# A fused attention and MoE kernel: a third quarter of one block in seven products, w_out loaded four neighbouring rows to a partition, and w_in's columns taken four apart

## The chip, the core and the metric

The kernel runs on one core of a Trainium2 chip. The metric is the device time of one execution in microseconds. The kernel before took 202.1 us, the median of three runs (201.06 to 202.36). TensorE (PE) multiplies, PEld is its loading of weights, VectorE (DVE), ScalarE (ACT) and GpSimd (POOL) work element by element, and SyncE (SP) issues DMAs; ScalarE and GpSimd issue DMAs as well.

## The reference

Linear attention with a decay per head over q, k, v of (4 batches, 8 heads, 768 positions, 64), in blocks of 64 positions, then a two-layer network over the 3072 tokens of 512 features.

```python
for b in range(nb):                              # blocks of 64 positions
    qb, kb, vb = (q[:, :, sl], k[:, :, sl], v[:, :, sl])
    intra = np.einsum('bhic,bhjc->bhij', qb, kb) * Dmask[None]
    intra = np.einsum('bhij,bhjd->bhid', intra, vb)
    inter = np.einsum('bhid,bhde->bhie', qb * lam_pow[None], kv_state)
    out[:, :, sl] = intra + inter
    kv_state = lam_block * kv_state + np.einsum('bhsd,bhse->bhde', kb * rev_pow[None], vb)
x = out.transpose(0, 2, 1, 3).reshape(B * S, H * D)      # 3072 x 512
h = x @ w_in                                             # 512 x 2048
return (h / (1 + np.exp(-h))) @ w_out                    # 2048 x 512
```

The hidden features (the 2048 columns of w_in and rows of w_out) may be taken in any order, as long as both matrices take the same.

## The kernel before

**Staging.** The 768 positions of a batch are six units of 128; with four batches there are 24 units of 128 tokens. They are worked in twelve sets of two units. For each set SyncE loads q, k and v (L411 for the first four sets, whose transfers carry runs of 512 bytes; L416 for the others), VectorE and ScalarE cast and scale them to bf16 (`kq`, `vd`), TensorE transposes (`tr`, L559 and L746; later sets by a DMA, L755), computes states `d_ps` (L581, L780) and scores `st_ps` (L634, L790), VectorE masks the scores (`st`), and TensorE makes the attention output `x_ps` (L660, L665, L812, L820). It is copied to `xt`, the transposed input of the first product. Between units the state is carried in `xf` and, as a block matrix, in `xe`.

**First product.** The tokens are in eight groups: four of 256 tokens (the first four sets) and four of 512 tokens. `product1` (L941 on) computes, for a group, the 16 tiles of 128 hidden features with four matmuls each, over the 512 input features (L958); ScalarE applies silu from PSUM into `g` (L973). For the last group, and for the half of the group before it named by `MIXED`, `product1_spared` (L1040 on) does a block product of 2 x 2 blocks with seven products in place of eight (`A11` to `A22` are quarters of w_in, `S1` to `S4` sums of them made by VectorE in `sums_of_w_in`, `B11` to `T4` quarters and sums of `xt`). One call of its loop, a quarter of a group, has seven products of four matmuls of 256 columns (L1079), the copies and additions between them (`m`, `h`) and four silus (L1103).

**Second product.** The first four units are done plainly (`product2_plain`, L996), the other 20 in five groups of four with seven products each (`products_of`, L1209), with sums of w_out's quarters made by VectorE and results stored from `osb` by ScalarE and SyncE.

**Weights.** `w_in_bf` holds w_in as 128 partitions x 4 x 2048 in bf16, `w_out_bf` holds w_out as 128 partitions x 16 x 512. GpSimd issues their DMAs, which cast from f32, in `load_w` (L437, L440): w_in in four chunks of 512 columns, w_out in four transfers of 512 rows. Before, tile number m of the hidden features is the 128 neighbouring columns 128 m to 128 m + 127 of w_in and the same rows of w_out, so that in each w_out transfer a partition takes four rows that lie 128 rows apart. `SEQUENCE` gives the order of all loads (`s` a set, `i` a chunk of w_in, with `a` and `b` for its halves, `o` a transfer of w_out, `@` a wait for an earlier load). On GpSimd the waits are small copies into `gate` (L391): the w_in loads wait for a load of the second set, the last two w_out transfers for k of the third set. Each set is loaded q first, then k, then v, for the first four sets.

**Order.** Nothing is issued in the order in which it is written. Every step is a task with a key, the engines that may do it, assumed costs, and the buffers it takes. `Planner.order` (L65) plays the tasks through once when the kernel is built, with assumed costs for engines and DMA transfers, gives each to an engine, and emits them in the order that results. On the chip each engine then runs its instructions in exactly that order; semaphores hold an instruction until its inputs are there. While TensorE has no task early on, the planner inserts fillers: four multiplications of the identity (L1295). The constants `LEAD`, `LAZY`, `HOLD`, `ON`, `POOLS` and others set keys, buffers and the planner's choices.

```python
w_in_r = moe_w_in.rearrange("(ko p) f -> p ko f", p=128)
w_out_r = moe_w_out.rearrange("(ko p) f -> p ko f", p=128)
...
nc.gpsimd.dma_start(out=w_in_bf[:, ks, cs], in_=w_in_r[:, ks, cs])
...
nc.gpsimd.dma_start(out=w_out_bf[:, ks, :], in_=w_out_r[:, ks, :])
...
nc.tensor.matmul(t[:, j, :], lhsT=w_in_bf[:, ko, 128 * (m1 + j):128 * (m1 + j) + 128],
                 rhs=xt[gi].tile[:, ko, :], start=ko == 0 and (j == 0 or len(kos) == KI),
                 stop=True, skip_group_check=True)
```

Of the kernel before, what the change touches and what calls it, by code (L numbers as in the profile page):

```python
# [11 lines left out]
AL = mybir.AluOpType  # L12
# [206 lines left out]
def kernel(  # L219
# [24 lines left out]
    PAIRED = 2  # L244
    SETS = [[(0, b), (1, b)] for b in range(B)] + [[(n, b), (n, b + 1)] for n in range(PAIRED, NB) for b in (0, 2)]
    GROUPS = SETS[:4] + [[(n, b) for b in range(B)] for n in range(PAIRED, NB)]
    FRESH, TURNED, ALONE, LEAD = 4, 6, 6, 4.25
    SEQUENCE = "s0 s1 i0a@1.1 i0b i1a i1b i2a i2b i3a i3b o0 o1 s2@1.0 o2 o3 s3 s4"
    POOLS = dict(bank=8, ra=3, rb=6, kq=3, kqT=3, vd=3, st=3, xe=6, xf=3, y=2, yf=2,
                 xt2=2, xt4=2, g=18, s=12, m=3, osb=3, one=3, two=8, att=6, sp=2)  # L250
    BY_POOL, PLAIN = (), 4
    CASTING, SUMS_AFTER, HURRY, SUMS_ON, HOLD, ONTO = 12, 16, 0.0, 9.0, 1, 24
    EARLY, PACE = 1.0, 1.0
    OPEN, FILLED, SCALED = 4, True, (1,)
    QUERIES = (0, 1, 2, 3)
# [177 lines left out]
    def load_w(key, what, j, part):  # L433
        def go(e):
            if what == "i":
                cs, ks = slice(512 * j, 512 * j + 512), {"": slice(0, 4), "a": slice(0, 2), "b": slice(2, 4)}[part]
                nc.gpsimd.dma_start(out=w_in_bf[:, ks, cs], in_=w_in_r[:, ks, cs])  # L437
            else:
                ks = slice(4 * j, 4 * j + 4)
                nc.gpsimd.dma_start(out=w_out_bf[:, ks, :], in_=w_out_r[:, ks, :])  # L440

        t = pool_task(add((key, 0), {"POOL": 0.8}, go, [], [], 0.5243 if part else 1.0486,
                          PIECE if part else LARGE, prior=pool_last[-1:], late=TAIL))
        wload.setdefault((what, j), []).append(t)
        for h in ("a", "b") if not part else part:
            wload[what, j, h] = t
# [233 lines left out]
    def prepare(si):  # L680
# [44 lines left out]
        def scale_v(e, j):  # L725
            if e != "DVE":
                for h in range(H):
# [4 lines left out]
        cv = [add((s - 0.8, 0), by_act("v", si, j), lambda e, j=j: scale_v(e, j),  # L732
                  deps=lv, bufs=[rs[2], o.vd]) for j in range(nb)]
        after("v", cv)
        o.cv, o.ck = cv, ck

# [110 lines left out]
    def after_first(o, t):  # L847

        n, bs, nb, s = o.n, o.bs, o.nb, o.s
        w = 512 * nb // 2  # L850

        def mask(e, p):
            tt(e, o.st_of()[:, p].rearrange("p b m i -> p (b m) i"), o.st_ps[p].tile.rearrange("p b m i -> p (b m) i"),
               tri[:, None, :].to_broadcast([128, nb * NP, 64]), AL.mult)

        o.masked = [add((s - 0.9, 0), {"DVE": 0.15 + w / 950}, lambda e, p=p: mask(e, p), deps=[t], bufs=[o.st_ps[p], o.st])
                    for p in range(2)]
        after("m", o.masked)
# [82 lines left out]
    def product1(gi, tiles=None):  # L941
# [5 lines left out]
        for m0 in tiles or range(0, KO, 2 * per):  # L947
            g = Buf("g")
            for half in range(2):
# [4 lines left out]
                def mm(e, kos, bank=bank, m1=m1):  # L954
                    t = tile_of(bank, [128, per, n], F32, "h_ps")
                    for j in range(per):
                        for ko in kos:
                            nc.tensor.matmul(t[:, j, :], lhsT=w_in_bf[:, ko, 128 * (m1 + j):128 * (m1 + j) + 128],  # L958
                                             rhs=xt[gi].tile[:, ko, :], start=ko == 0 and (j == 0 or len(kos) == KI),
                                             stop=True, skip_group_check=True)  # L960

# [78 lines left out]
    def product1_spared(gi, wbufs, wdone, parts):  # L1040
# [23 lines left out]
        for jp in parts:  # L1064
# [20 lines left out]
            def keep(pool, deps, P=P, bank_of=bank_of):  # L1085
                b = Buf(pool)
                t = add((u0 - eager, 5), {"ACT": 0.6, "DVE": 0.69}, lambda e: copy(e, tile_of(b, [128, 2, 256], F32, "m"), bank_of(P)),
                        deps=deps, bufs=[b, P])
                return b, t

            narrow = {"22": Buf("vd" if closing else "y"), "12": Buf("st" if closing else "y")}

            def h_of(x, narrow=narrow):
                return tile_of(narrow[x], [128, 2, 256], F32, "h")

            def total_of(x, kept, deps, R=R, bank_of=bank_of, h_of=h_of, narrow=narrow):
                return add((u0 - eager, 5), {"DVE": 0.7}, lambda e: tt(e, h_of(x), bank_of(R), kept.tile, AL.add), deps=deps,
                           bufs=[R, kept, narrow[x]])

            def silu(dst, src, deps, bufs):  # L1100
                def go(e):
# [10 lines left out]
            m6 = product(2, P, "S2", "T2", False, [c1])  # L1112
            b2, c2 = keep("kqT" if closing else "kq", [m6])
            m5 = product(3, R, "S1", "T1", True, [s11])
            m7 = product(4, P, "S3", "T3", False, [c2])
            b3, c3 = keep("xf" if closing else KEPT, [m7])
            e22 = total_of("22", b3, [m5, c3])
            m4 = product(5, P, "A22", "T4", False, [c3])
            m3 = product(6, R, "S4", "B22", False, [e22])
            e12 = total_of("12", b2, [m3, c2])  # L1120
            s22 = silu((high, hi), lambda h_of=h_of: h_of("22"), [e22], [narrow["22"]])
            s21 = silu((high, lo), lambda P=P, f=bank_of: f(P), [m4], [P])
            s12 = silu((low, hi), lambda h_of=h_of: h_of("12"), [e12], [narrow["12"]])
# [208 lines left out]
```

## Time and profile before

| | |
|---|---|
| median of three runs | 202.1 us (201.06 to 202.36) |
| profiled execution, its own time | 201.3 us |
| span of its instructions | 199.6 us |
| TensorE matmuls | 187.6 us busy, 2607 |
| weight loads | 143.7 us busy, 2623 |
| VectorE / ScalarE / GpSimd | 145.6 / 122.3 / 13.2 us busy |
| DMA | 32.89 MB in 84894 packets |
| queue 1 (SyncE), queue 0 (GpSimd), queue 10 (ScalarE) | 75074, 4288, 5506 packets |

Busy times are shares of one execution's span. Matmuls are pipelined, and their ends are modelled: the pace of TensorE is read from how many matmuls stand in a piece of the chain and how long the piece is, and not from the duration of one. In the chain of waits each piece is given by its start, its length and what ran in it. In a timeline a piece has its start, its length, the engine, the line, the operation and what it writes and reads; what stands in brackets is how long the engine was idle before it, and what ended that. The stretches give, for each, its length and the busy time of each engine in it with the number of instructions, the granted TensorE clock as a share of full speed, the share of the DMA engines and GB/s.

### The profile page before, as it was taken

Reading aid. Unit: us, or ns where it says so; the run is one execution under the profiler, and the core shown is the slowest. Engines: PE = TensorE matmul, PEld = TensorE weight load, DVE = VectorE, ACT = ScalarE, POOL = GpSimd, SP = SyncE. Lnnn points to the kernel's source line nnn. Section 1 sums busy time; section 2 is a strip of 40 time slices with the busy share of each in tenths; the row PEclk is TensorE's granted clock in tenths of the full one; section 3 lists DMA queues with packets and bytes.
Section 4 is the critical chain, followed back from the end, with each engine's and each line's share of the span. In section 5 each row is a group of like instructions: output and inputs, shape, how many; then the busy total and the mean of one; then the engine's idle time right before and its main releaser. Section 6 shows DMA issues by size and latency. Waiting matters only on the chain.

```text
span 199.6 us, 6042 instructions
## 1 busy us (share of the span) xinstructions
PE 187.6 (94%) x2607; PEld 143.7 (72%) x2623; DVE 145.6 (73%) x302; ACT 122.3 (61%) x230; POOL 13.2 (7%) x35
## 2 busy tenths in 40 slices
PE   0699999999999998999999999999999999999993
PEld 0588687547777884667778747488887588888882
DVE  7899220279997999949999774999979763837611
ACT  2867767319896846647291574834795849765320
POOL 6086003000000000000000000000000000000000
PEclk9999999999999999999999999999999999999999
DMA  5999999999999999999989999802911001003213
GB/s 154 290 241 194 213 216 217 275 216 246 248 276 211 220 251 166 266 193 219 275 183 218 219 251 184 186 7 72 143 53 56 3 0 53 3 6 104 95 38 131
DMA packets 84894, 32.89 MB, mean 165 GB/s; under 512 B 62852, under 2 KB 84356, under 8 KB 84868
## 3 DMA queue, kind: packets, MB, share of 16 engines
q1 hardware_dynamic: 75074, 22.55, 56.0%
q0 software_dynamic: 4288, 4.20, 12.8%
q10 hardware_dynamic: 5506, 5.77, 8.9%
q8 instruction: 20, 0.33, 0.7%
q14 instruction: 6, 0.05, 0.1%
HBM read 27.26 MB, written 6.29 MB: 168 GB/s over the span
## 4 chain that ended last, share of the span: by engine, by line
PE 79%; DMA 8%; DVE 8%; POOL 1%; SPq 1%; issue 1%; ACT 0%; POOLq 0%
PE o_ps L1209 29%; PE h_ps L958 27%; PE h_ps L1079 9%; PE o_ps L996 6%; DMA w_in_bf<-in_moe_w_in_dram 4%; DMA raw<-in_q_dram 4%; PE x_ps L820 2%; PE d_ps L780 1%; DVE st L369 1%; DVE kq L369 1%; SPq L411 1%; POOL w_in_bf L437 1%; DVE xe L364 1%; PE st_ps L790 1%; PE x_ps L812 1%; PE tr L559 1%
## 5 line engine op out<-in xcount | busy, mean ns | idle before, releaser
L958 PE MATMUL h_ps<-xt,w_in_bf 128*128 128x256 bf16 (+1 forms) x407 | 66.2, 313 | 1.6 <-ACT xe L362 0.6
L958 PEld LDWEIGHTS <-w_in_bf 128*128 128x128 bf16 x416 | 39.3, 98 | 21.8 <-DVE xt L364 1.2
L973 ACT ACTIVATE g<-h_ps 128x512 bf16<-128x512 f32 x72 | 41.6, 596 | 16.8 <-PE h_ps L958 13.4
L1209 PEld LDWEIGHTS <-g 128*128 128x128 bf16 x320 | 31.2, 98 | 4.7
L1209 PEld LDWEIGHTS <-s 128*128 128x128 bf16 x240 | 23.4, 98 | 3.2
L369 DVE TENSOR_TENSOR st<-st_ps,tri 128x512 bf16<-128x512 f32 x32 | 20.3, 682 | 3.9 <-PE st_ps L790 3.9
L369 DVE TENSOR_TENSOR osb<-o_ps,m 128x512 f32<-128x512 f32 (+1 forms) x18 | 10.7, 599 | 15.8 <-ACT m L362 8.0
L362 ACT ACTIVATE m<-o_ps 128x512 f32<-128x512 f32 (+1 forms) x18 | 9.4, 522 | 18.8 <-PE o_ps L1209 18.7
L369 DVE TENSOR_TENSOR kq<-raw,lam_q 128x512 bf16<-128x512 f32 x24 | 15.9, 685 | 5.1 <-DMA raw<-in_q_dram 4.8
L369 DVE TENSOR_TENSOR vd<-raw,lam_v 128x512 bf16<-128x512 f32 x24 | 15.8, 686 | 4.7 <-DMA raw<-in_v_dram 4.6
L1209 PE MATMUL o_ps<-w_out_bf,s 128*128 128x256 bf16 x160 | 19.1, 273 | 0.0
L1209 PE MATMUL o_ps<-wsum,g 128*128 128x256 bf16 x160 | 18.9, 273 | 0.0
L1209 PE MATMUL o_ps<-w_out_bf,g 128*128 128x256 bf16 x160 | 18.6, 273 | 0.0
L362 ACT ACTIVATE xt<-x_ps 128x512 bf16<-128x512 f32 x16 | 9.8, 642 | 9.0 <-PE x_ps L820 6.1
L996 PE MATMUL o_ps<-w_out_bf,g 128*128 128x512 bf16 x57 | 14.1, 380 | 0.6 <-issue 0.3
L369 DVE TENSOR_TENSOR h<-h_ps,m 128x512 f32<-128x512 f32 x12 | 8.3, 690 | 8.0 <-PE h_ps L1079 3.7
L362 ACT ACTIVATE kqT<-tr 128x512 bf16<-128x512 bf16 x20 | 10.8, 595 | 2.3 <-PE tr L559 2.2
L362 ACT ACTIVATE kq<-raw 128x512 bf16<-128x512 f32 x16 | 9.9, 625 | 1.9 <-DMA raw<-in_k_dram 1.9
L1079 PEld LDWEIGHTS <-wsum 128*128 128x128 bf16 x96 | 9.4, 98 | 1.1
L996 PEld LDWEIGHTS <-g 128*128 128x128 bf16 x64 | 5.9, 98 | 5.5
L369 DVE TENSOR_TENSOR s<-g 128x512 bf16<-128x512 bf16 x20 | 8.3, 420 | 2.1 <-ACT g L973 1.4
L1209 PE MATMUL o_ps<-wsum,s 128*128 128x256 bf16 x80 | 9.6, 273 | 0.0
(93 smaller groups left out, 241.4 us busy)
## 6 DMA issues: line engine op xcount, KB each, us to landing
raw<-in_q_dram SPq DMA_DIRECT2D x12, 512.0 KB, 7.2
raw<-in_k_dram SPq DMA_DIRECT2D x12, 512.0 KB, 7.7
raw<-in_v_dram SPq DMA_DIRECT2D x12, 512.0 KB, 8.1
out_dram<-osb ACTq DMA_DIRECT2D x20, 256.0 KB, 3.9
w_in_bf<-in_moe_w_in_dram POOLq DMA_DIRECT2D x8, 256.0 KB, 9.4
w_out_bf<-in_moe_w_out_dram POOLq DMA_DIRECT2D x4, 512.0 KB, 14.5
out_dram<-osb ACTq DMA_DIRECT2D x4, 128.0 KB, 1.7
out_dram<-osb SPq DMA_DIRECT2D x4, 128.0 KB, 1.7
```

What stands on the lines that cost most here:

```text
L362: nc.scalar.activation(o, i, AF.Copy)
L364: nc.vector.tensor_copy(o, i)
L369: (nc.vector if e == "DVE" else nc.gpsimd).tensor_tensor(o, a, b, op=op)
L411: nc.sync.dma_start(out=rs[i].tile.rearrange("p h e d -> p h (e d)"), in_=x[i])
L437: nc.gpsimd.dma_start(out=w_in_bf[:, ks, cs], in_=w_in_r[:, ks, cs])
L559: nc.tensor.transpose(t[:, m, a], o.kq_of()[:, i, m, a], ident)
L820: nc.tensor.matmul(x_of(c)[:, j, m, :], lhsT=o.xe[c].tile[:, (bs[0] + j) % 2, m, :], rhs=o.kqT_of()[:, 1, j, m, halves[c]], start=False, s ...
L958: nc.tensor.matmul(t[:, j, :], lhsT=w_in_bf[:, ko, 128 * (m1 + j):128 * (m1 + j) + 128], rhs=xt[gi].tile[:, ko, :], start=ko == 0 and (j = ...
L973: nc.scalar.activation(t[:, half * per:half * per + per], bank.tile, AF.Silu)
L996: nc.tensor.matmul(t, lhsT=g.tile[:, j, 128 * gp:128 * gp + 128], rhs=w_out_bf[:, ko, :], start=(ko == 0), stop=(ko == KO - 1))
L1079: nc.tensor.matmul(t[:, j, :], lhsT=W[w]()[:, k2, f:f + 128], rhs=X(r)[:, k2, :], start=first and j == 0 and k2 == 0, stop=True, skip_grou ...
L1209: nc.tensor.matmul(t[:, i_, :], lhsT=src(j)[:, k2, 128 * r:128 * r + 128], rhs=W[w]()[:, 2 * j + k2, :], start=first and i_ == 0 and j == ...
```

## The change

Hidden features change places. In a chunk of 512, tile m now holds the columns m % 4, m % 4 + 4, m % 4 + 8 and so on of w_in, and the four rows of w_out that a partition takes in one transfer are neighbours in memory. Both products use the same order, so the result is that of the reference. The sums of w_in's quarters keep their layout and are read with the same step of four.

The third quarter of the group before the last (`MIXED`) is done in seven products. The order of w_in's chunks is 0, 3, 1, 2, the last two in one transfer each. Some constants of the planner change. The scaling of the carried state (`next_states`) may go to ScalarE for units 3 and 4 of a batch. `scale_pair` and the branch for `SHARED` are added but not used, as `WHOLE` and `SHARED` are empty.

```diff
-    FRESH, TURNED, ALONE, LEAD = 4, 6, 6, 4.25
-    SEQUENCE = "s0 s1 i0a@1.1 i0b i1a i1b i2a i2b i3a i3b o0 o1 s2@1.0 o2 o3 s3 s4"
+    FRESH, TURNED, ALONE, LEAD = 4, 6, 6, 4.5
+    SEQUENCE = "s0 s1 i0a@1.1 i0b i3a i3b i1 i2 o0 o1 s2@1.0 o2 o3 s3 s4"
     POOLS = dict(bank=8, ra=3, rb=6, kq=3, kqT=3, vd=3, st=3, xe=6, xf=3, y=2, yf=2,
-                 xt2=2, xt4=2, g=18, s=12, m=3, osb=3, one=3, two=8, att=6, sp=2)
+                 xt2=2, xt4=2, g=18, s=12, m=3, osb=3, one=4, two=8, att=6, sp=2)
-    CASTING, SUMS_AFTER, HURRY, SUMS_ON, HOLD, ONTO = 12, 16, 0.0, 9.0, 1, 24
+    CASTING, SUMS_AFTER, HURRY, SUMS_ON, HOLD, ONTO = 12, 16, 0.0, 9.0, 0, 24
-    LAZY, FINE, SAFE, EASY, TAIL, SURE = 2.0, True, 1.3, -0.22, 0.9, 1.5
+    LAZY, FINE, SAFE, EASY, TAIL, SURE = 0.5, True, 1.3, -0.22, 0.9, 1.5
-    MIXED, APART, KEPT = (0, 1), 1, "yf"
-    EAGER, CALM, ON = 10.0, 1.0, 0.0
+    MIXED, APART, KEPT = (0, 1, 2), 1, 'yf'
+    EAGER, CALM, ON = 10.0, 1.0, 2.0
+    SHARED = ()
+    WHOLE = ()
+    RATED = (3, 4)
...
-    w_out_r = moe_w_out.rearrange("(ko p) f -> p ko f", p=128)
+    w_out_r = moe_w_out.rearrange("(j p k) f -> p j k f", p=128, k=4)
+
+    def columns(m):
+        return slice(512 * (m // 4) + m % 4, 512 * (m // 4) + 512, 4)
...
-                nc.gpsimd.dma_start(out=w_out_bf[:, ks, :], in_=w_out_r[:, ks, :])
+                nc.gpsimd.dma_start(out=w_out_bf[:, ks, :], in_=w_out_r[:, j])
...
-        tf = add((s - 0.9, 4), {"DVE": dcost}, lambda e: tt(e, xf_of(), y.tile, rate, AL.mult),
-                 deps=[ty], bufs=[y, xf_n])
+        def next_states(e):
+            if e == "DVE":
+                tt(e, xf_of(), y.tile, rate, AL.mult)
+                return
+            for m in range(NP):
+                by_rate(e, xf_of()[:, :, m], y.tile[:, :, m], lam_be[:, m:m + 1])
+
+        tf = add((s - 0.9, 4), {"DVE": dcost, **({"ACT": 1.1} if n in RATED else {})}, next_states, deps=[ty], bufs=[y, xf_n])
...
-                            nc.tensor.matmul(t[:, j, :], lhsT=w_in_bf[:, ko, 128 * (m1 + j):128 * (m1 + j) + 128],
+                            nc.tensor.matmul(t[:, j, :], lhsT=w_in_bf[:, ko, columns(m1 + j)],
...
-                        f = 128 * (2 * jp + j)
+                        f = columns(2 * jp + j)
...
-                            nc.tensor.matmul(t[:, j, :], lhsT=W[w]()[:, k2, f:f + 128], rhs=X(r)[:, k2, :],
+                            nc.tensor.matmul(t[:, j, :], lhsT=W[w]()[:, k2, f], rhs=X(r)[:, k2, :],
```

More of the change, by code (lines that the diff above doesn't have):

```diff
@@ L730, in scale_v, with scale_pair @@
             tt(e, vd_of()[:, j], rs[2].tile[:, j * H:j * H + H, :], lam_v[:, :, None].to_broadcast([128, H, 64]), AL.mult)
-        cv = [add((s - 0.8, 0), by_act("v", si, j), lambda e, j=j: scale_v(e, j),
-                  deps=lv, bufs=[rs[2], o.vd]) for j in range(nb)]
+        def scale_pair(e, m):
+            dst = vd_of()[:, :, 2 * m:2 * m + 2]
+            src = rs[2].tile.rearrange("p (b h) d -> p b h d", h=H)[:, :, 2 * m:2 * m + 2]
+            if e == "DVE":
+                tt(e, dst, src, lam_v[:, None, 2 * m:2 * m + 2, None].to_broadcast([128, nb, 2, 64]), AL.mult)
+                return
+            for h in range(2):
+                by_rate(e, dst[:, :, h], src[:, :, h], lam_v[:, 2 * m + h:2 * m + h + 1])
+        if si in WHOLE:
+            cv = [add((s - 0.8, 0), {"ACT": 0.64, "DVE": 0.42}, lambda e, m=m: scale_pair(e, m), deps=lv, bufs=[rs[2], o.vd]) for m in range(NP)]
+        else:
+            cv = [add((s - 0.8, 0), by_act("v", si, j), lambda e, j=j: scale_v(e, j),
+                      deps=lv, bufs=[rs[2], o.vd]) for j in range(nb)]
         after("v", cv)
@@ L1083, in product, with keep, total_of @@
                            bufs=held + [x, one, two] + ([wbufs[w]] if w in wbufs else []))
-            def keep(pool, deps, P=P, bank_of=bank_of):
+            def keep(pool, deps, bank, bank_of=bank_of):
                 b = Buf(pool)
-                t = add((u0 - eager, 5), {"ACT": 0.6, "DVE": 0.69}, lambda e: copy(e, tile_of(b, [128, 2, 256], F32, "m"), bank_of(P)),
-                        deps=deps, bufs=[b, P])
+                t = add((u0 - eager, 5), {"ACT": 0.6, "DVE": 0.69}, lambda e: copy(e, tile_of(b, [128, 2, 256], F32, "m"), bank_of(bank)),
+                        deps=deps, bufs=[b, bank])
                 return b, t
-            narrow = {"22": Buf("vd" if closing else "y"), "12": Buf("st" if closing else "y")}
+            narrow = {"22": Buf("vd" if closing else "y")}
+            if gi not in SHARED:
+                narrow["12"] = Buf("st" if closing else "y")
             def h_of(x, narrow=narrow):
                 return tile_of(narrow[x], [128, 2, 256], F32, "h")
-            def total_of(x, kept, deps, R=R, bank_of=bank_of, h_of=h_of, narrow=narrow):
-                return add((u0 - eager, 5), {"DVE": 0.7}, lambda e: tt(e, h_of(x), bank_of(R), kept.tile, AL.add), deps=deps,
-                           bufs=[R, kept, narrow[x]])
+            def total_of(x, kept, deps, bank, bank_of=bank_of, h_of=h_of, narrow=narrow):
+                return add((u0 - eager, 5), {"DVE": 0.7}, lambda e: tt(e, h_of(x), bank_of(bank), kept.tile, AL.add), deps=deps,
+                           bufs=[bank, kept, narrow[x]])
             def silu(dst, src, deps, bufs):
@@ L1111, in product1_spared @@
             s11 = silu((low, lo), lambda R=R, f=bank_of: f(R), [m2], [R])
[L1112 to L1123, printed above, removed]
+            if gi in SHARED:
+                m6 = product(2, P, "S2", "T2", False, [c1])
+                m5 = product(3, R, "S1", "T1", True, [s11])
+                b5, c5 = keep(KEPT if not closing else "xf", [m5], R)
+                e4 = add((u0 - eager, 5), {"DVE": 0.7}, lambda e, P=P, R=R, b5=b5, f=bank_of: tt(e, f(R), f(P), b5.tile, AL.add), deps=[m6, c5],
+                         bufs=[P, R, b5])
+                m7 = product(4, P, "S3", "T3", False, [e4])
+                m3 = product(6, R, "S4", "B22", False, [e4])
+                e22 = total_of("22", b5, [m7], P)
+                s22 = silu((high, hi), lambda h_of=h_of: h_of("22"), [e22], [narrow["22"]])
+                m4 = product(5, P, "A22", "T4", False, [e22])
+                s21 = silu((high, lo), lambda P=P, f=bank_of: f(P), [m4], [P])
+                s12 = silu((low, hi), lambda R=R, f=bank_of: f(R), [m3], [R])
+            else:
+                m6 = product(2, P, "S2", "T2", False, [c1])
+                b2, c2 = keep("kqT" if closing else "kq", [m6], P)
+                m5 = product(3, R, "S1", "T1", True, [s11])
+                m7 = product(4, P, "S3", "T3", False, [c2])
+                b3, c3 = keep("xf" if closing else KEPT, [m7], P)
+                e22 = total_of("22", b3, [m5, c3], R)
+                m4 = product(5, P, "A22", "T4", False, [c3])
+                m3 = product(6, R, "S4", "B22", False, [e22])
+                e12 = total_of("12", b2, [m3, c2], R)
+                s22 = silu((high, hi), lambda h_of=h_of: h_of("22"), [e22], [narrow["22"]])
+                s21 = silu((high, lo), lambda P=P, f=bank_of: f(P), [m4], [P])
+                s12 = silu((low, hi), lambda h_of=h_of: h_of("12"), [e12], [narrow["12"]])
```

2 lines of the change are left out of this document (added).

## The prediction

> **What bounds the kernel now.** I read the busy shares first, then the same engines cut at the places where the chain of waits changes its kind, then the chain.
>
> ```profile
> PE 187.6 (94%) x2607; PEld 143.7 (72%) x2623; DVE 145.6 (73%) x302; ACT 122.3 (61%) x230; POOL 13.2 (7%) x35
> ```
>
> ```profile
> 0.00:22.30 22.30, 15.05 (x315) 12.47 (x315) 18.49 (x45) 14.76 (x31) 11.36 (x32) 1.00 1.05 219
> 22.30:76.00 53.70, 53.09 (x805) 40.11 (x812) 36.10 (x68) 35.38 (x66) 1.86 (x3) 1.00 1.15 235
> 76.00:196.50 120.50, 119.45 (x1488) 91.08 (x1496) 90.56 (x189) 72.12 (x133) 0.00 (x0) 1.00 0.59 126
> 196.50:199.60 3.10, 0.00 (x0) 0.00 (x0) 0.45 (x2) 0.00 (x0) 0.00 (x0) 0.86 0.27 89
> ```
>
> The second group's columns after the stretch are its length and the busy time of PE, PEld, DVE, ACT and POOL. From 22.3 to 196.5 us TensorE is idle for 0.61 + 1.05 = 1.7 us: this is TensorE time, and whatever makes TensorE work longer or wait there is added to the end in full. The chain says what a matmul costs and what starts the dense part.
>
> ```profile
> 13.32 8.96 DMA w_in_bf<-in_moe_w_in_dram
> ...
> 35.33 0.45 PE tr L559 x8
> 35.78 0.44 PE h_ps L958 x4
> 36.21 4.32 PE o_ps L996 x20
> ...
> 82.86 3.49 PE o_ps L1209 x32
> ```
>
> The fourth w_in transfer lands at 22.28; until then TensorE runs out of work. After it, a 256-column matmul with its own weight load comes every 3.49/32 = 109 ns, a 512-column one every 4.32/20 = 216 ns, and a transpose, also with a weight load of 128 columns, every 0.45/8 = 56 ns. So a unit-step load fits into 56 ns, and behind a 256-column matmul 109 - 56 = 53 ns of cover are left.
>
> **1. The third quarter of block 4 in seven products.** Removed: 16 matmuls of 512 columns, 16 x 216 = 3.46 us. Added: 28 of 256 columns, 28 x 109 = 3.05 us. TensorE saves 0.4 us. Added on the evacuation side: three copies of about 0.6 us ("m<-h_ps 128x512" took 599 ns, "h_ps<-h_ps" 583) and two additions of 690 ns, 3.2 us in all. They lie in 140 to 160 us, where VectorE is busy 8.4 + 8.4 and ScalarE 8.2 + 7.2 of 20 us, 7.8 us free together. Hidden; if a bank came back late, the product after it would wait at most about one such copy, 0.6 us. Two "xf" scalings move from VectorE (0.69 each) to ScalarE as four pieces each; by the 414 ns of a 64x256 activation they are under 1.7 us per scaling, and ScalarE has 39% free. Zero, with the same bound of 0.6.
>
> **2. w_in's columns four apart.** No instruction is added by this. In the built order of the changed kernel all 596 weight loads from w_in_bf and its sums take every fourth column (8 bytes apart): 452 stand before a 256-column matmul, 144 before a 512-column one. No weight load of the trace has a step, so the cost is bounded: below by nothing (nothing can be gained, as loads are covered already), above by the step of four costing four times the 56 ns, 224 ns. With a load of L ns the cost is 452 x (L - 109) + 144 x (L - 216), each term only where positive: nothing up to 109 ns, 1.4 us at 112 (twice 56), 53 us at 224. I take nothing. The Trainium skill's "TensorE: Matmul & The Clock Gate", section "LDWEIGHTS (loading the stationary operand)", gives columns / 1.2, 107 ns for 128 columns; by the 56 ns here loads go twice as fast, and by that price the sum would still be nothing. Its "SBUF — State Buffer" (note on cachelines) says that a read needs two hits on a 16-byte line, so that eight bf16, and not only four, can be stepped for free; no row here can show it.
>
> **3. w_out with four neighbouring rows in a partition.** The four transfers bring the same bytes, but in the built order their destination is one run of 2048 elements per partition in place of four of 512: 512 packets in place of 2048, four times as large. TensorE waits for a DMA only 0.2 us after 22 us, so faster transfers gain nothing by themselves. But there is a loser. I counted the trace's packets from 27.8 to 31.4 us: 498 of w_out's 1024 bytes on queue 0, 498 of 512 bytes on queue 1, which brings k of the third set. The queues take turns packet by packet, whatever the size. With packets four times as large the share of queue 1 falls.
>
> Before: k of the third set sends its 1024 packets from 24.2 to 31.4; at 27.8, when w_out begins, about 500 are left. After: the first two w_out transfers have 16 packets for each of 16 engines. A w_out packet of 1 KB (2 KB read) took 96 ns, a cycle with the other queue's packet 3.6 us x 16 / 498 = 116 ns, so some 20 ns more. The large packet: 342 ns by the 8192-byte row of queue 14 (307 its shortest), 384 by four times 96. A cycle is 320 to 400 ns, I take 360, nearest to queue 14's row plus 20: 16 x 0.36 = 5.8 us, in which k moves 256 packets. The other 243 then go alone at the 596 per us seen from 36 to 38 us: 0.4 us. k is through at 27.8 + 5.8 + 0.4 = 34.0 in place of 31.4, 2.6 us later (1.9 to 3.2). Who waits for it:
>
> ```profile
> 32.92 0.43 DVE L364 CAST kq<-raw 128x512 bf16<-128x512 f32 x1 [5.82 <-DMA raw<-in_k_dram]
> ...
> 33.82 0.63 ACT L362 ACTIVATE kq<-raw 128x512 bf16<-128x512 f32 x1
> ...
> 35.17 0.61 PE L559 MATMUL tr<-ident,kq 128*128 128x128 bf16 x8
> ```
>
> VectorE's cast starts as k lands (32.89), ScalarE's after a silu. With k at 35.5, ScalarE's cast ends at 36.1 and the transposes start at 36.2 in place of 35.33. TensorE keeps its order, so it waits there: 0.9 us (0.2 to 1.5). Behind the transposes stand 4 matmuls of the second block and 20 of the second product, all delayed with it; on ScalarE the copies of the transposes and a silu. v of the same set ends about where it did (35.9), as the bytes are the same. The gate on GpSimd that waits for k (L391, then 33.33) releases the last two w_out transfers 2.6 us later. They landed at 42.37 and 46.84; the first is needed at 42.5, now 43.4. Its packets started 4.4 us after the issue, those of the first w_in transfer 2.0; between these it lands at 41.7 to 44.5, a further wait of 0 to 1.1 us, taken as nothing.
>
> **4. The opening.** w_in's chunks now come 0, 3, 1, 2, the first two in halves, the last two whole. On queue 0 the bytes per transfer are the same up to the fourth, so 22.28 stays. The built order does four matmuls (0.44 us) fewer before the wait at 22.28; then 36 matmuls (3.9 us) are ready from chunks 0 and 3, to 26.25, and chunk 1 is complete at 25.95 (the landing of the sixth half), chunk 2 at 29.47 for use at 30.2. To the transposes at 35.33 that is 100 matmuls x 109 + 0.45 + 1.73 (eight of 512) = 35.4, where 96 with some holes reached 35.33. Nothing. On ScalarE the scaling "xe<-xf" (0.84) now stands before the second "xt"; the first matmuls of block 0 may start up to 0.8 later, before 22.28: of the 5.3 us from 16.94 on, 28 matmuls (3.05) and two bursts (0.57 and 0.33) fill 3.95, so 1.4 us are idle or fillers.
>
> **5. The rest of the planner's settings** reorder evacuations between 60 and 165 us. The only hole there is 0.57 us at 76.0, where TensorE waits for VectorE's "xt" behind "xf"; that order of VectorE is the same in the built kernel. Nothing, at best -1.7 us if every hole after 22.3 closed.
>
> **Sum:** -0.4 + 0.9 = +0.5 us. The profiled execution took 201.3 us (span 199.6, 1.7 around it), 0.8 under the median 202.1 of the three runs; by the same distance the changed kernel's median is 201.3 + 0.5 + 0.8 = 202.6 us.
>
> **Rivals.**
> - *Strided loads too slow (slower).* Place: all 596 loads from w_in. It decides from 109 ns per load on; past 113.5 ns it costs over 2 us. At 112 the time is 202.6 + 1.4 = 204.0, at 224 about 255. For it: no strided load in the trace, and 128 columns every 109 ns leave it no more than half speed. Against: 53 ns of cover. Chance 0.14.
> - *k is not pushed back.* The rows of 8 KB are cut into the old packets, or k comes in time: then only part 1 is left, 202.1 - 0.4 = 201.7. For it: no packet of queue 0 larger than 1 KB is in the trace. Chance 0.2. This is also the case in which the change of w_out does not do what it says.
> - *k pushed back, and the last two w_out transfers late as well:* 1.5 + 1.1 - 0.4 = +2.2, 204.3. For it: 42.37 against 42.5 is a margin of 0.1 us. Against: after a wait at 35 everything is later. Chance 0.1.
> - *Holes close:* the 0.57 us at 76 and the small ones go with part 1's 0.4: 202.1 - 1.7 - 0.4 = 200.0 at best, 201 more likely. Chance 0.06.
>
> **How the numbers follow.** The forecast has 0.5; its own terms (0.2 to 1.5 for k, up to 0.6 for an evacuation) give 201.6 to 203.3. The range of 201.0 to 204.5 takes in the forecast, the unpushed k and the late w_out; it leaves out most of the strided case and half of the holes, under 2 in 10. One per cent is 2.0 us, about what a measurement tells from no change: faster needs under 200.1, only the end of the last rival, 0.04; slower needs over 204.1, most of the strided case (0.12), some of the late w_out (0.06) and 0.02 of the forecast: 0.2. The same: 0.76.
>
> **What would show it.** Packets of queue 0: 2048 of 1 KB and 512 of 4 KB. k of the third set landing near 35.5 and a TensorE wait of about 0.9 before the transposes at 36.2; L958 and L1079 matmuls of 256 columns still every 109 ns; 16 matmuls of 512 columns fewer. Wrong if these matmuls come slower, if k lands by 34.5, or if new holes show after 76 us.

## The result, and the profile after

The changed kernel takes 215.99 us, the median of six runs (214.82 to 216.95); the kernel before took 202.03 (201.06 to 202.41) beside it. The ratio is 1.0692, with an interval of 1.0658 to 1.0726: slower by 7%. The forecast was 202.6, so 13.4 us came from something that none of its terms held.

The page of the changed kernel: the span, the busy shares, the slices of TensorE and of its granted clock, and the group of the first product's matmuls.

```profile
span 214.2 us, 6085 instructions
PE 188.7 (88%) x2625; PEld 153.0 (71%) x2639; DVE 146.1 (68%) x305; ACT 126.1 (59%) x238; POOL 10.8 (5%) x33
PE   0792009999999999999999999999999999999993
PEclk9999557999999999999999999999999999999999
L985 PE MATMUL h_ps<-xt,w_in_bf 128*128 128x256 bf16 (+1 forms) x393 | 64.3, 315 | 15.0 <-DMA w_in_bf<-in_moe_w_in_dram 13.4
```

TensorE is busy for 188.7 us, 1.1 more than before, while the span grew by 14.6. So it did not work much longer, it stood still, and the third row says where: in slices four to six, between 16 and 32 us. The last row names what ended it: one wait of 13.4 us for w_in. In the last two of these slices the granted clock is at half. The timeline of TensorE (start, length, what stood before it in brackets) has it in two lines:

```profile
18.01 0.27 PE L985 MATMUL h_ps<-xt,w_in_bf 128*128 128x256 bf16 x1 [0.72 <-ACT xt L370]
31.68 3.24 PE L985 MATMUL h_ps<-xt,w_in_bf 128*128 128x256 bf16 x15 [13.41 <-DMA w_in_bf<-in_moe_w_in_dram]
```

One matmul of the first product ran, and the second came 13.4 us later, 0.13 us after the sixth and last w_in transfer landed (31.55). The 15 matmuls then took 3.24/15 = 216 ns each, where 109 is the pace elsewhere. The stretches show the same (length, then busy time of PE, PEld, DVE, ACT and POOL, the granted clock, DMA share, GB/s):

```profile
18.00:20.00 2.00, 0.27 (x1) 0.00 (x0) 1.86 (x5) 0.00 (x0) 0.00 (x0) 1.00 1.11 188
20.00:22.00 2.00, 0.00 (x0) 0.00 (x0) 0.65 (x2) 0.00 (x0) 0.00 (x0) 0.75 1.19 216
22.00:24.00 2.00, 0.00 (x0) 0.00 (x0) 0.00 (x0) 0.00 (x0) 0.00 (x0) 0.50 1.20 216
...
32.00:34.00 2.00, 2.00 (x12) 1.39 (x11) 0.00 (x0) 0.00 (x0) 0.00 (x0) 0.50 1.05 218
34.00:36.00 2.00, 2.00 (x43) 1.49 (x42) 0.47 (x1) 1.74 (x4) 0.22 (x2) 0.83 1.12 315
```

From 22 us on all engines are idle while the DMA engines stay as full as in the kernel before (216 GB/s against 217 from 22 to 24 us). The last w_in transfer landed 2.1 us later than before (31.55 against 29.47), and not 13: the data did not come late, TensorE asked for it too early. The chain of waits (start, length, what ran) shows that the path to the end led through it, where before it had gone through the fourth w_in transfer, 8.96 us from its issue:

```profile
14.83 16.72 DMA w_in_bf<-in_moe_w_in_dram
31.55 0.14 issue
31.68 3.24 PE h_ps L985 x15
...
36.94 6.65 PE h_ps L985 x60
...
50.13 0.45 PE tr L567 x8
```

After that nothing differs by much: the transposes that the forecast watched start 14.8 us later (50.13 against 35.33), the last matmul 14.4 later (210.65 against 196.21).

**Where the wait comes from.** The landings that TensorE's instructions wait for can be read in the built program. For the first block (16 matmuls, four tiles with the rows ko = 0 to 3 of `w_in_bf`) they are, with C0a for the first half of chunk 0 (rows 0 and 1), C0b for its second half (rows 2 and 3), C1 for all of chunk 1:

| kernel | ko = 0 | ko = 1 | ko = 2 | ko = 3 |
|---|---|---|---|---|
| before | C0a | none new | C0b | none new |
| changed | C0a | **C1, C2, C3a** | C0b | C3b |
| before, with the two new layouts (below) | C0a | **C1a, C2a, C3a** | C0b | C1b, C2b, C3b |
| changed, chunk outermost in `w_in_bf` (below) | C0a | none new | C0b | none new |
| changed, one row per transfer (below) | own row | own row | own row | own row |

The matmuls with ko = 1 read columns 0 to 511 of row 1, which C0a brings. No byte of C1, C2 or C3a is read. The listed waits fit one rule, which is inferred from them: the framework that sets them compares the read with the region that a transfer writes; a region of several rows is a block of 512 columns repeated every 2048 elements, and a read with a step of four that lies *between* two rows of such a region is taken to touch it. Row 1's read lies between rows 0 and 1 of every other chunk; row 0's lies ahead of them all, and is exempt. With a unit step the comparison is exact. How the framework does the comparison was not looked at; that the wait is not needed follows from the addresses, and what it depends on is what the experiments vary.

### The profile page after: what moved, and what is told of

It reads as the page before. It is cut to its first block, busy times and chain, and to the rows that moved or that the text cites. A ratio compares the mean times of both kernels' runs of the same rounds, so it can differ in the third digit from the quotient of the medians.

```text
span 214.2 us, 6085 instructions
## 1 busy us (share of the span) xinstructions
PE 188.7 (88%) x2625; PEld 153.0 (71%) x2639; DVE 146.1 (68%) x305; ACT 126.1 (59%) x238; POOL 10.8 (5%) x33
## 3 DMA queue, kind: packets, MB, share of 16 engines
q0 software_dynamic: 2720, 4.19, 11.3%
## 4 chain that ended last, share of the span: by engine, by line
PE 74%; DMA 12%; DVE 7%; POOL 2%; SPq 1%; issue 1%; ACT 1%; DVEq 0%; POOLq 0%
PE h_ps L985 26%; PE o_ps L1253 25%; PE h_ps L1106 10%; DMA w_in_bf<-in_moe_w_in_dram 8%; PE o_ps L1023 6%; DMA raw<-in_q_dram 3%; POOL w_in_bf L445 2%; PE x_ps L841 2%; PE d_ps L801 1%; DVE st L377 1%; DVE kq L377 1%; SPq L419 1%; DVE xe L372 1%; PE st_ps L811 1%; DMA out_dram<-osb 1%
## 5 line engine op out<-in xcount | busy, mean ns | idle before, releaser
L985 PE MATMUL h_ps<-xt,w_in_bf 128*128 128x256 bf16 (+1 forms) x393 | 64.3, 315 | 15.0 <-DMA w_in_bf<-in_moe_w_in_dram 13.4
L985 PEld LDWEIGHTS <-w_in_bf 128*128 128x128 bf16 x400 | 43.8, 115 | 29.1 <-issue 14.4
L1000 ACT ACTIVATE g<-h_ps 128x512 bf16<-128x512 f32 x68 | 39.5, 597 | 28.7 <-PE h_ps L985 28.1
L1253 PEld LDWEIGHTS <-g 128*128 128x128 bf16 x320 | 31.1, 98 | 4.6
L372 DVE CAST xt<-x_ps 128x512 bf16<-128x512 f32 x8 | 5.6, 704 | 19.8 <-PE x_ps L668 14.9
L370 ACT ACTIVATE m<-o_ps 128x512 f32<-128x512 f32 (+1 forms) x17 | 8.8, 517 | 15.6 <-PE o_ps L1253 15.5
L377 DVE TENSOR_TENSOR h<-h_ps,m 128x512 f32<-128x512 f32 x14 | 9.7, 689 | 8.8 <-ACT m L370 4.7
L1106 PEld LDWEIGHTS <-wsum 128*128 128x128 bf16 x112 | 12.3, 113 | 0.2
L1132 ACT ACTIVATE g<-h 128x512 bf16<-128x512 f32 x14 | 8.8, 628 | 3.5 <-DVE h L377 3.2
L1106 PE MATMUL h_ps<-xsum,wsum 128*128 128x256 bf16 x84 | 10.8, 273 | 0.0
L1132 ACT ACTIVATE g<-h_ps 128x512 bf16<-128x512 f32 x14 | 8.3, 596 | 3.1 <-PE h_ps L1106 3.0
```

The lines of the kernel that those rows point to most:

```text
L370: nc.scalar.activation(o, i, AF.Copy)
L372: nc.vector.tensor_copy(o, i)
L985: nc.tensor.matmul(t[:, j, :], lhsT=w_in_bf[:, ko, columns(m1 + j)], rhs=xt[gi].tile[:, ko, :], start=ko == 0 and (j == 0 or len(kos) == K ...
L1000: nc.scalar.activation(t[:, half * per:half * per + per], bank.tile, AF.Silu)
L1106: nc.tensor.matmul(t[:, j, :], lhsT=W[w]()[:, k2, f], rhs=X(r)[:, k2, :], start=first and j == 0 and k2 == 0, stop=True, skip_group_check= ...
L1132: nc.scalar.activation(o, src(), AF.Silu)
```

## The experiments

Ratios are against the kernel before, run beside each.

**Undo both layouts.**

```diff
-    w_out_r = moe_w_out.rearrange("(j p k) f -> p j k f", p=128, k=4)
+    w_out_r = moe_w_out.rearrange("(j k p) f -> p j k f", p=128, k=4)
     def columns(m):
-        return slice(512 * (m // 4) + m % 4, 512 * (m // 4) + 512, 4)
+        return slice(128 * m, 128 * m + 128)
```

> The changed kernel with both layouts undone (tile m is again 128 neighbouring columns of w_in, w_out's rows again 128 apart), everything else kept: the third quarter in seven products, the chunk order, the planner's settings. Theory (the loss is a wait that the step of four brings into the program: the second matmul of the first block waits for the transfers of all chunks): the first product starts near 17 us as before, and the time is 202.0 - 0.4 = 201.6 us (201.0 to 202.6). Rival (the planner's settings or the chunk order cost the 14 us): it stays at 214 us or more. Rival (w_in's transfers themselves are slower, 31.55 against 29.47 for the last): 203 to 205.

Measured: 202.38 us (ratio 1.0012, 0.9983 to 1.0042). The loss belongs to the layouts; the third quarter, the order of the chunks and the planner's settings together make no difference that can be measured.

**Keep both layouts, store w_in chunk by chunk.** `w_in_bf` becomes 128 x 4 chunks x 4 rows x 512, so that a transfer is one piece and no read of a chunk lies between rows of another. Step four, large packets and the order of every engine's instructions stay; the reads of `w_in_bf` and the sums of its quarters follow the new layout (not shown).

```diff
-    w_in_bf = const.tile([128, KI, DFF], BF16, name="w_in_bf")
+    w_in_bf = const.tile([128, 4, KI, 512], BF16, name="w_in_bf")
...
-                nc.gpsimd.dma_start(out=w_in_bf[:, ks, cs], in_=w_in_r[:, ks, cs])
+                nc.gpsimd.dma_start(out=w_in_bf[:, j, ks, :], in_=w_in_r[:, ks, cs])
```

> The changed kernel with w_in held chunk by chunk in SBUF (128 x 4 chunks x 4 x 512 in place of 128 x 4 x 2048). The step of four, w_out's four neighbouring rows, the chunk order and the settings stay; only the bytes of one chunk now lie in one piece, so that the first block's matmuls wait for their own chunk alone. Theory (false wait): the 14 us are gone, and what is left is what the prediction summed, 202.6 us (201.6 to 203.3), with k of the third set landing near 35.5. Rival (the strided load itself is slow, its records are 115 ns in place of 98): still over 210 us, with matmuls of 256 columns later than every 109 ns. Rival (w_in lands late): 203 to 206, with TensorE idle before 22 to 26 us.

Measured: 202.95 us (1.0045, 1.0018 to 1.0072), 13.0 below the changed kernel. The timeline of TensorE has the first block whole, and short waits for its own chunks:

```profile
18.00 2.16 PE L985 MATMUL h_ps<-xt,w_in_bf 128*128 128x256 bf16 x16 [0.72 <-ACT xt L370]
...
21.50 0.63 PE L985 MATMUL h_ps<-xt,w_in_bf 128*128 128x256 bf16 x4 [0.77 <-DMA w_in_bf<-in_moe_w_in_dram]
...
36.63 0.77 PE L567 MATMUL tr<-ident,kq 128*128 128x128 bf16 x8
```

**The layouts alone, on the kernel before.** The lines of the two layouts, nothing else.

> The kernel before with the two layouts alone (w_in's columns four apart, w_out with four neighbouring rows); all loads in the old order, all chunks in halves. Theory (false wait): the second matmul now waits for the first halves of all chunks, and matmuls of the second half for all second halves, which landed at 27.66 and 29.47 before; TensorE does 9 matmuls in place of some 90 by then, so 10 to 12 us more, 212 to 214 us. Rival (the whole transfers of chunks 1 and 2 or the new chunk order are needed for the loss): 202 to 203 us.

Measured: 214.43 us (1.0612, 1.0565 to 1.066), a little over the 212 to 214 expected, which counted the idle time and not the half clock behind it. Its waits are those of the third row of the table, and the landings agree: its seventh transfer, C3a, landed at 28.46, and the second matmul started at 28.60.

```profile
17.18 0.27 PE L961 MATMUL h_ps<-xt,w_in_bf 128*128 128x256 bf16 x1
28.60 3.54 PE L961 MATMUL h_ps<-xt,w_in_bf 128*128 128x256 bf16 x15 [11.15 <-DMA w_in_bf<-in_moe_w_in_dram]
```

So neither the order of the chunks nor their coming whole makes the loss; with halves the last landing that the second matmul waits for is at 28.46 in place of 31.55, and the loss is 12.3 us in place of 14.0.

**The wait without any step.** The first of these runs, with unit-step loads, gets one multiplication that really reads the last chunk.

```diff
+                    if gi == 0 and m1 == 0 and 0 in kos:
+                        nc.tensor.matmul(t[:, 0, 0:128], lhsT=w_in_bf[:, 1, 1024:1152], rhs=ident,
+                                         start=True, stop=True, skip_group_check=True)
                     for j in range(per):
```

> e1_unit (both layouts as before, every weight load with unit step) plus one 128-column multiplication ahead of the first matmul of the first product, whose weights are 128 columns of the sixth w_in transfer; its result is overwritten. So the first block really reads what the changed kernel only waits for, and no load has a step. Theory (the wait alone makes the loss): TensorE is idle from about 17.5 until the sixth transfer lands at 30 to 31.5, and the next 15 matmuls come at half pace; e1's 202.4, plus 12 to 13.5 of idle time less the 1.9 that e1 idles there, plus 1.6: 214.5 to 215.7. Rival (the stepped loads, or bank conflicts between them and DMA writes, have a part in the loss): clearly less, under 212.

Measured: 215.13 us (1.0659, 1.0633 to 1.0685), inside the 214.5 to 215.7 that the wait alone gives. In its timeline:

```profile
30.34 0.29 PE L984 MATMUL h_ps<-ident,w_in_bf 128*128 128x128 bf16 x1 [12.89 <-DMA w_in_bf<-in_moe_w_in_dram]
30.41 3.62 PE L987 MATMUL h_ps<-xt,w_in_bf 128*128 128x256 bf16 x16
```

With no stepped read in the kernel the time is the changed kernel's to 0.9 us, and here the sixth transfer landed 1.3 us earlier (30.29), so nothing has to be looked for in the reads themselves.

**One row per transfer.** The layout and the step of the changed kernel, 16 transfers in place of six.

```diff
-                nc.gpsimd.dma_start(out=w_in_bf[:, ks, cs], in_=w_in_r[:, ks, cs])
+                for k in range(ks.start, ks.stop):
+                    nc.gpsimd.dma_start(out=w_in_bf[:, k, cs], in_=w_in_r[:, k, cs])
```

> The changed kernel with each w_in transfer issued row by row (16 transfers of one row of w_in_bf and 512 columns, in place of six of two or four rows); layout of w_in_bf, step of four and w_out are the changed kernel's. In the built program the second matmul of the first block then waits for its own row alone. Theory (the wait arises where a stepped read lies between the rows of a transfer of several rows): the idle 13.4 us are gone, 203 us, 202.5 to 205, as ten more issues of 0.5 to 0.8 us on GpSimd may bring w_out later. Rival (step-of-four reads of w_in_bf are held up in this layout whatever the transfers): 214 or more.

Measured: 206.79 us (1.0238, 1.0193 to 1.0284). The long wait is gone with the same reads, as the rule has it, but 206.8 is outside 202.5 to 205. Its timeline shows where the rest went, in waits of another kind:

```profile
21.81 0.30 PE L986 MATMUL h_ps<-xt,w_in_bf 128*128 128x256 bf16 x1 [0.79 <-DMA w_in_bf<-in_moe_w_in_dram]
22.88 0.52 PE L986 MATMUL h_ps<-xt,w_in_bf 128*128 128x256 bf16 x3 [0.77 <-DMA w_in_bf<-in_moe_w_in_dram]
...
25.21 0.30 PE L986 MATMUL h_ps<-xt,w_in_bf 128*128 128x256 bf16 x1 [0.93 <-DMA w_in_bf<-in_moe_w_in_dram]
25.85 6.63 PE L986 MATMUL h_ps<-xt,w_in_bf 128*128 128x256 bf16 x59 [0.34 <-DMA w_in_bf<-in_moe_w_in_dram]
...
45.38 0.32 PE L590 MATMUL d_ps<-vd,kq 64*64 64x64 bf16 x16 [1.16 <-DVE vd L377]
```

The last row of C3 landed at 25.81, C3b in the chunk-by-chunk kernel at 23.29: from 16 to 20 us queue 0 moved 289 packets of 1 KB, there 470, which fits small transfers that do not keep their queue full. v of the third set landed at 44.61, there at 37.96, and TensorE waits for it at 45. I had counted the issues on GpSimd and taken the landings of w_in as unchanged.

**Neighbouring rows of w_out alone.** Unit step for w_in, large packets for w_out.

> w_out with four neighbouring rows in a partition, but w_in's columns unit-step, otherwise the changed kernel. The output is not the reference's, as the two matrices then take the hidden features in different orders; the work is the same. Against the kernel with both layouts undone it prices w_out's large packets alone. Theory (queues take turns packet by packet): k of the third set lands about 2.6 us later than there, TensorE waits before the third set's transposes, +0.9 us (0.2 to 1.5). Rival (TensorE has enough work in front of the transposes): within 0.2 us.

Measured: 202.98 us (1.0061, 1.003 to 1.0093). Against both layouts undone that is 0.6 us more by the medians and 0.5% by the ratios, whose intervals overlap, for an expected 0.9 (0.2 to 1.5): the sign and the size rest on the traces. The timeline around the second set of transposes, first with both layouts undone:

```profile
35.35 0.63 ACT L370 ACTIVATE kq<-raw 128x512 bf16<-128x512 f32 x1
36.26 0.61 PE L567 MATMUL tr<-ident,kq 128*128 128x128 bf16 x8
```

With the large packets:

```profile
36.10 0.63 ACT L370 ACTIVATE kq<-raw 128x512 bf16<-128x512 f32 x1 [0.99 <-DMA raw<-in_k_dram]
36.10 0.43 DVE L372 CAST kq<-raw 128x512 bf16<-128x512 f32 x1 [5.53 <-DMA raw<-in_k_dram]
36.59 0.76 PE L567 MATMUL tr<-ident,kq 128*128 128x128 bf16 x8 [0.38 <-DVE kq L372]
```

k of the third set landed at 36.08 in place of 33.86, the casts now wait for it and TensorE for a cast. The first two w_out transfers came 0.9 and 1.6 us earlier (32.95 and 35.69 against 33.81 and 37.33), and nobody had waited for them.

**What a stepped load costs.** In the first of these runs, with unit-step loads, the sums of w_in were read with a larger step, 8 elements and then 16.

> The disputed load by itself: the changed kernel with both layouts undone, but the 112 weight loads from the sums of w_in's quarters take every eighth column (16 bytes apart) within their row. The output is not the reference's; the number of matmuls is the same. In the changed kernel the step of four left the pace at 109 ns and lengthened a load's record from 98 to 114 ns. Theory (a load that takes one element of each 16 bytes is slower than one that takes two): the record passes 140 ns and these 256-column matmuls come later than every 109 ns. Rival (the step costs the same whatever it is): about 115 ns and 109 ns.

> As the run with a step of eight, with every sixteenth element (32 bytes apart) over both rows of a sum. The output is not the reference's. Theory (one element per 16 bytes is the worst case): as with a step of eight. Rival (the cost grows with the step): twice the excess of the step of eight over 98 ns.

Measured: 202.49 and 203.93 us. The groups of these loads, after the first bar their busy time and the mean ns of one. With step 1:

```profile
L1106 PEld LDWEIGHTS <-wsum 128*128 128x128 bf16 x112 | 11.0, 98 | 1.5
```

Step 4, the changed kernel:

```profile
L1106 PEld LDWEIGHTS <-wsum 128*128 128x128 bf16 x112 | 12.3, 113 | 0.2
```

Step 8:

```profile
L1106 PEld LDWEIGHTS <-wsum 128*128 128x128 bf16 x112 | 12.8, 144 | 0.4
```

Step 16:

```profile
L1106 PEld LDWEIGHTS <-wsum 128*128 128x128 bf16 x112 | 12.9, 145 | 0.4
```

The record grows, 98, 113, 144, 145, and the 256-column matmuls of that line keep 109 ns from start to start in all four, none over 113. So each side of the first forecast had half of it: the record passed 140 ns, as the theory had it, and the pace did not change, as the rival had it. A record of 145 ns inside a pace of 109 means that records overlap, so their length is no price. The 203.93 of the second is one execution whose fourth w_in transfer landed at 24.65 (22.89 in the first); no change of pace in the stages of these loads goes with it.

**How much of the loss is the clock.** The changed kernel with 228 multiplications of the identity ahead of the first product, so that TensorE works through the wait.

```diff
+                    if gi == 0 and m1 == 0 and 0 in kos:
+                        for i in range(228):
+                            nc.tensor.matmul(t[:, 0, 0:128], lhsT=ident, rhs=ident,
+                                             start=True, stop=True, skip_group_check=True)
                     for j in range(per):
```

> The changed kernel with 228 multiplications of the identity in front of the first matmul of the first block, 228 x 56 ns = 12.8 us, so that TensorE works through most of the wait for w_in and comes out of it at the full clock. In the changed kernel the first 15 matmuls after the wait came every 216 ns in place of 109, at a granted clock of about a half. Theory (the 13 us are the wait, 13.6 us, and the clock after it, 15 x 107 ns = 1.6 us): the first product goes on at the same moment, near 31.6 us, at 109 ns, and the time is 216.0 - 1.6 = 214.4 us (213.9 to 214.9). Rival (the low clock costs nothing that the later work does not give back): 216 us.

Measured: 214.15 us (1.0627, 1.0578 to 1.0676), 1.8 less than the changed kernel, with 228 multiplications more. Its timeline of TensorE:

```profile
17.39 13.14 PE L985 MATMUL h_ps<-ident 128*128 128x128 bf16 x228
30.36 1.95 PE L988 MATMUL h_ps<-xt,w_in_bf 128*128 128x256 bf16 x16
```

Its granted clock is 1.00 throughout, and the first block runs at 109 ns. From the pace the half clock costs 15 x (216 - 109) = 1.6 us; the intervals of the two ratios overlap, so the times alone do not settle it, and in this profiled execution the last w_in transfer landed 1.2 us earlier (30.37) as well.

**The third quarter alone.** The kernel before with one constant.

```diff
-    MIXED, APART, KEPT = (0, 1), 1, "yf"
+    MIXED, APART, KEPT = (0, 1, 2), 1, "yf"
```

> The kernel before with the third quarter of block 4 in seven products and nothing else: the old layouts, chunk order and settings. Theory (TensorE time is end time): 16 matmuls of 512 columns less and 28 of 256 more, 0.4 us less, ratio 0.998 to the kernel before. Rival (three more copies and two more additions come late and stop TensorE by as much): 1.000 or more.

Measured: 201.14 us over twelve runs, ratio 0.9959 (0.9938 to 0.9981): the fastest of all, and ahead of both kernels. The trace gives the size better than the times, since openings differ by about 1 us between executions. The timeline has the end of the hole at 76 us and the last multiplications; the kernel before:

```profile
76.65 2.12 PE L958 MATMUL h_ps<-xt,w_in_bf 128*128 128x512 bf16 x8 [0.57 <-ACT xe L362]
...
194.79 1.69 PE L1209 MATMUL o_ps<-w_out_bf,s 128*128 128x256 bf16 x14
```

With the third quarter:

```profile
77.89 0.82 PE L958 MATMUL h_ps<-xt,w_in_bf 128*128 128x512 bf16 x3 [0.57 <-ACT xe L362]
...
195.41 1.91 PE L1209 MATMUL o_ps<-w_out_bf,s 128*128 128x256 bf16 x16
```

196.48 - 76.65 = 119.83 us before, 197.32 - 77.89 = 119.43 with it: 0.40 less. By the ratio the gain is 0.8 us (0.4 to 1.3); the half of it that the trace does not show is within that interval.

**The old opening.** Both layouts undone, and the old order of the chunks with two of the planner's settings (`LEAD`, `LAZY`).

> The changed kernel with both layouts undone and with the old chunk order, LEAD and LAZY as well; the third quarter and the other settings stay. In the run with the layouts undone alone, the first product started at 18.0 us in place of 16.9, since ScalarE does a scaling of the state in front of the second copy to xt, and TensorE then waited 1.2 us for a w_in transfer with four matmuls fewer done. Theory (this opening eats what the seven products save): with the old opening 0.5 to 1 us faster than that run, ratio 0.996 to 0.999 to the kernel before. Rival (the later settings cost it): no faster than that run, ratio 1.001 or more.

Measured: 201.61 us (1.0001, 0.9971 to 1.003). By medians 0.8 us less than with the new opening, by ratios 0.1%, and neither the 0.996 to 0.999 of the theory nor the 1.001 of the rival: not settled. In its profile the first product starts with 0.1 us of idle time ahead of it in place of the 0.7 us wait for `xt`, and waits 0.3 us for w_in in place of 1.2.

**Before again.** The same kernel, to see how much its opening varies.

> The kernel before, unchanged, for a second trace of its opening: how far the landing of the fourth w_in transfer (22.28 us) and of k of the third set (32.89 us) move from one execution to the next. In the runs with unit-step columns the fourth transfer landed between 22.37 and 24.65 us. Theory (these landings vary by about 1 us with the same program): 22 to 24 us here. Rival (the new chunk order makes them late): 22.3 again.

Measured: 201.93 us. The fourth w_in transfer landed at 23.05 (22.28 in the execution shown before), and TensorE was idle for 1.0 us before it, where the first trace had 0.2. The trace from which the forecast was worked out had an early opening.

## Why the prediction was wrong

**Step 2 failed, and not in its price.** "No instruction is added by this" was read from the order of the matmuls and loads, and their order is indeed the same with the layouts and without them. What changed was what they wait for. The built program has one instruction of TensorE more than with both layouts undone: a semaphore wait for C1 and C2 ahead of the second w_in matmul (whose weight load waits for C3a as well), set by the framework, and it cost 13.4 us of idle time. "With a load of L ns the cost is" was a search for the price of the read alone, with bounds from 0 to 53 us, and behind 256-column matmuls that price is the zero that I took: the pace stays at 109 ns for steps of 4, 8 and 16. The Trainium skill's "SBUF — State Buffer" (the note on cachelines) lets eight bf16 be stepped for free; the runs agree for 4 and 8 in pace, and 16, beyond its limit, cost no pace behind a 256-column matmul either.

**Step 4 failed with it.** "36 matmuls (3.9 us) are ready from chunks 0 and 3" and "chunk 1 is complete at 25.95" took for granted that a matmul waits for its own chunk alone. In the changed kernel the second matmul waits for the sixth transfer. "The bytes per transfer are the same up to the fourth, so 22.28 stays" was one execution: the fourth landing was at 24.39 in the changed kernel, at 22.4 to 24.7 in the profiles of the other kernels with halves, and at 23.05 in the second profile of the kernel before.

The loss can be followed against the chunk-by-chunk kernel, which has the same instructions in the same order, by the starts of the same matmul in the two traces. The second matmul comes 13.6 us later. Behind the first block the delay is 14.8, as the 15 matmuls take 1.6 us longer and the chunk-by-chunk kernel has itself waited some 0.4 us by then. Its waits for the two halves of chunk 3 bring it to 13.9 and 13.4, its wait for the second set of transposes, with small waits of the changed kernel on the way, to 13.2. The last matmul ahead of the hole at 76 us starts at 90.61 against 77.44, 13.2 later, and the medians differ by 13.0.

**The rival "strided loads too slow"** had the right edit and the right sign, and not the mechanism: its lever was the duration of 596 loads, and the loss came once, ahead of one matmul.

**Step 3 held, with half of the wait it gave.** Packets of queue 0: 2720 in place of 4288, as 512 large ones take the place of 2048 small, and 32 packets of 4 bytes fewer come with two transfers fewer; a 4096-byte packet took 322 ns, the median (estimated 342 to 384). k landed at 35.67 in the changed kernel (forecast 35.5), 2.2 us later in the clean comparison (forecast 2.6, 1.9 to 3.2). TensorE waited 0.4 to 0.5 us for it (forecast 0.9, 0.2 to 1.5). In the changed kernel itself this cost nothing, because TensorE came to the transposes at 50: one wait hid the other. In the chunk-by-chunk kernel, where the step can act, the time was 202.95 for a forecast of 202.6. That these two are so close is in part luck: the wait for k was half of its term, and the opening, which step 4 put at nothing, had idle times of 0.7 us for `xt` and 1.1 for w_in, where the trace before had 0.1 and 0.2 (0.1 and 1.0 in its second profile).

**Step 1 held**: 0.40 in the trace for a forecast of 0.4, and no evacuation became late on TensorE's path. **Step 5 held**: the hole at 76 us stays in every kernel (0.5 to 0.6 us of idle time), though it ends with ScalarE's `xe` behind VectorE's `xf`, not with "xt" as I wrote.

## What to carry to other kernels

When the shape of an access changes, compare the waits of the built program and not only the order of its instructions: a semaphore wait that was not written stands in no diff of the kernel and in no list of its matmuls and loads, and here one of them cost 13 us where the access itself, behind 256-column matmuls, cost nothing. A read with a step in a buffer that several transfers fill, each with several rows, is the place to look; a layout in which each transfer writes one piece removed the wait and kept the change, which is then no faster than the kernel before (1.0045). And the waits of 11 to 13 us on TensorE were followed by 3 to 6 us at half clock.

## What the runs showed of the hardware

- The granted clock fell from 1.00 to 0.50 at about 21.0 us, 2.7 us after the last matmul (0.75 in the stretch 20 to 22 us, one matmul at 18.0 being the last), and stayed at 0.50 to about 34.7 (0.83 in the stretch 34 to 36), 3.0 us after TensorE resumed at 31.68. That time is not fixed: with the layouts alone the same stretches have 0.77 and 0.82 and TensorE was back at 28.60, with the true read 0.85 and 0.74 and 30.34, so that the half clock went on for 6.1 and 4.7 us. From fall to rise it is 13.6 to 13.7 us in all three. The Trainium skill's "TensorE: Matmul & The Clock Gate" (Part 1: The HAM clock gate) gives about 3.4 us of activity for the way up, whatever the number of matmuls, in a window that it calls free-running; the traces agree, with 3.0 to 6.1 us, from about one such window to less than two.
- The two load queues took turns packet by packet with packets of 4096 bytes as well: from 30 to 32 us 113 of queue 0 (88 of them of 4096 bytes, 322 ns each) and 116 of queue 1 (114 of them of 512 bytes). So larger packets take time from the neighbour queue: k of the third set, on queue 1, landed 2.2 us later, and with large packets alone TensorE waited for it.
- The record of a weight load grows with its step (98, 113, 144, 145 ns for 1, 4, 8, 16), without any effect on the pace of 256-column matmuls.
- The same kernel's fourth w_in transfer landed 0.8 us apart in two executions, as much as most terms of the forecast.
